# Linear attention and two feed-forward layers: q and k turned by VectorE's block transposes, projected as 32-row tiles in four single PSUM banks

## The chip, the cores and the metric

The kernel runs on one core of a Trainium2 chip. A core has a matrix engine (TensorE, PE in the profile, with PEld for its weight loads), a vector engine (VectorE, DVE), an activation engine (ScalarE, ACT), a general engine (GpSimd, POOL) and a queue engine that here only starts transfers (SyncE, SP). Each runs its own list of instructions in order and waits for the others at semaphores. Matmul results land in PSUM, which has eight banks of 128 x 512 fp32. The metric is the device time of one launch in microseconds (us).

## The reference

```
phi(x):  proj = x @ w_phi                       # 64 -> 128 features
         proj = proj - max|proj|  (per token)
         [exp(proj), exp(-proj)]
kv  = phi(k)^T v ;  z = sum phi(k)              # per batch (4) and head (8)
att = phi(q) kv / (phi(q) z + 1e-6)             # 576 tokens, head width 64
x   = att as (4*576) x 512
x   = (sigmoid(x w_gate) * (x w_val)) w_out     # 512 -> 1536 -> 512
out = max(0.01 h, h) w_out2,  h = x w_in2       # 512 -> 2048 -> 512
```

q, k, v and w_phi are fp32. The feed-forward weights come as 64-bit floats and are decoded on the chip into a high and a low part, and each product of these layers is three matmuls (`mm3`: high by high, high by low, low by high).

## The kernel before

**Stages.** The attention stage handles 16 pairs (a batch and two heads). Of a pair's 576 tokens, 512 are the main part, four tokens (J = 4) to a partition, and 64 are a remainder that two pairs share. After it comes the feed-forward stage; its first matmuls write `ps_u`. So that TensorE has more to do, the attention stage also takes in the first part of the gated layer for batches 0 to 2 (`gated_unit`, its chunk 0, 72 units M of three matmuls, written to `ps_g` and `ps_d`), and ten weight blocks are decoded in it (L104 to L111, five VectorE instructions each, tiles `e`, `m`, `raw`).

**A pair, step by step.** `load_kq`, `load_rem` and `load_v` fetch k, q, the remainder and v. TensorE transposes k and q, four 128 x 128 blocks each, into a PSUM pair of banks (`turn`, L408, `ps_t`); ScalarE or VectorE copies them to SBUF as x (L425, L428, and `evict` at L377 and L379, shared out by the string `XC`). `proj` (L396) multiplies x by w_phi: a head's 64 rows are one row tile, two heads stand in the array, and a matmul writes 128 columns of `ps_p`; `wbd` holds w_phi once for each head. VectorE takes the largest absolute value of each token (`absmax`, L383, 128 x 1024 for k and again for q) and subtracts it (`centre`, L388, tiles `t` and `tq`). ScalarE takes the two exponentials of k (`ka`, L455). TensorE transposes q's values (L500, L502, `ps_q`, `ps_r`) and ScalarE takes their exponentials (`qf`). `kv` (L526, L528) sums over the tokens, `kc` copies the sum to SBUF, and `om` (L545, L548, `ps_n`) multiplies it by q's features. `rc` and `nm` (L553 to L560) divide, `ot` (L573, L574, `ps_o`) transposes back, `xs` copies to `rb` (string `UC`), and `xh`, `xl` split it into high and low parts.

**Order.** The string `ORDER` lists the pieces, and under `manual_schedule` each engine gets its instructions in that order:

```
for piece in ORDER.split():
    nm = piece.rstrip("0123456789")
    if nm == "d": ...            # one step of a weight decode
    elif nm == "f": ...          # fetch the next raw weights
    elif nm in gated: gated[nm].popleft()()     # M t s h l c
    else: fns[nm](pair[int(piece[len(nm):])])
```

The eight warm-up matmuls on the identity (`ps_w`, L305 to L307) stand ahead of it.

**Banks.** Three pools of a pair of banks (`ps_p`, given out by the string `picks`) and two single banks (`ps_a`) serve the attention stage; the feed-forward stage opens pools of its own (L655 to L657).

## Time and profile before

| | us |
|---|---|
| median of 3 runs | 982.39 (981.71 to 983.8) |
| the profiled run's own time | 982.46 |
| its span in the trace | 980.7 |
| TensorE busy | 963.9 (98%) |
| VectorE busy | 732.1 (75%) |
| ScalarE busy | 470.6 (48%) |
| GpSimd busy | 166.6 (17%) |

The span is what the trace covers; 1.8 us of the profiled run lie around it. Busy times are sums over instructions. Matmuls overlap in the array, so what a run of matmuls takes is read from the start of one group to the start of the next, not from the duration of a record. An fp32 matmul leaves two records, so 16 matmuls read as x32.

### The profile page before, as it was taken

To read this page: it belongs to the slowest core of one execution; us is meant where nothing else is said; L and a number is where in the kernel's file an instruction comes from. 1 tells how busy PE (TensorE), PEld (TensorE's weight loads), DVE (VectorE), ACT (ScalarE), POOL (GpSimd) and SP (SyncE) were. 2 spreads that over 40 slices of the span, in tenths; PEclk is the share of its full clock that TensorE was granted. 3 is DMA by queue.
4 is the path that set the end of the run, shared out by engine and by line. 5 is a ranking of instruction groups with operands and counts; after the bars stand their busy time and mean duration, and the time that the engine had idled before them with its cause. 6 is when DMAs were issued, how large, how long until landed. Compare 5 with 4: busy or idle time off the path is not lost.

```text
span 980.7 us, 17543 instructions
## 1 busy us (share of the span) xinstructions
PE 963.9 (98%) x7040; PEld 820.7 (84%) x7040; DVE 732.1 (75%) x1226; ACT 470.6 (48%) x828; POOL 166.6 (17%) x228
## 2 busy tenths in 40 slices
PE   8999999999999999999999999999999999999998
PEld 7888889888888888888888887888888888888886
DVE  5898768625983838839839899987979797978545
...
GB/s 172 170 160 142 91 138 97 25 66 259 295 334 111 152 250 50 260 200 77 282 145 150 193 214 189 135 225 76 213 45 236 25 252 40 222 80 114 88 138 139
DMA packets 110177, 153.25 MB, mean 156 GB/s; under 512 B 62480, under 2 KB 65168, under 8 KB 110096
## 3 DMA queue, kind: packets, MB, share of 16 engines
...
## 4 chain that ended last, share of the span: by engine, by line
PE 76%; DVE 2%; issue 1%; POOL 0%; ACT 0%; DVEq 0%
PE ps_u L52 14%; PE ps_u L53 14%; PE ps_u L54 14%; PE ps_p L53 11%; PE ps_p L52 11%; PE ps_p L54 11%; DVE acc L738 1%; PE ps_n L545 0%; PE ps_d L52 0%; PE ps_g L52 0%; PE ps_g L54 0%; PE ps_g L53 0%; DVE w L807 0%; PE ps_d L53 0%; PE ps_d L54 0%
## 5 line engine op out<-in xcount | busy, mean ns | idle before, releaser
L908 DVE TENSOR_TENSOR q<-ps_u,q 128x512 f32<-128x512 f32 x160 | 109.6, 686 | 60.6 <-PE ps_u L54 54.1
L53 PE MATMUL ps_u<-xl,w 128*128 128x512 f32 (+1 forms) x432 | 151.4, 350 | 0.3 <-DVE xl L743 0.3
L52 PE MATMUL ps_u<-xh,w 128*128 128x512 f32 (+1 forms) x432 | 151.2, 350 | 0.0
L54 PE MATMUL ps_u<-xh,w 128*128 128x512 f32 (+1 forms) x432 | 151.1, 350 | 0.0
L978 DVE TENSOR_TENSOR acc<-acc,ps_p 128x512 f32<-128x512 f32 x126 | 86.1, 683 | 39.3 <-PE ps_p L54 38.7
L52 PE MATMUL ps_p<-w,gh 128*128 128x512 f32 x288 | 112.2, 390 | 0.0
L53 PE MATMUL ps_p<-w,gh 128*128 128x512 f32 x288 | 112.1, 390 | 0.0
L54 PE MATMUL ps_p<-w,gl 128*128 128x512 f32 x288 | 111.8, 389 | 0.0
L868 POOL DMA_DIRECT2D w<-td x88 | 48.5, 557 | 356.5 <-PE ps_u L54 344.7
L52 PE MATMUL ps_u<-w 128*128 128x512 f32 x256 | 100.2, 391 | 1.6 <-DVE q L908 1.6
L53 PE MATMUL ps_u<-w 128*128 128x512 f32 x256 | 99.9, 390 | 0.0
L54 PE MATMUL ps_u<-w 128*128 128x512 f32 x256 | 99.7, 389 | 0.0
L735 POOL DMA_DIRECT2D accd<-w x72 | 63.6, 894 | 189.5 <-ACT w L734 144.5
L53 PEld LDWEIGHTS ps_u<-xl,w 128*128 128x128 f32 x432 | 81.7, 189 | 11.7 <-DVE xl L743 0.5
L52 PEld LDWEIGHTS ps_u<-xh,w 128*128 128x128 f32 x432 | 81.7, 189 | 11.4
L54 PEld LDWEIGHTS ps_u<-xh,w 128*128 128x128 f32 x432 | 81.7, 189 | 10.9
L774 ACT ACTIVATE q<-q 128x512 f32<-128x512 f32 x48 | 30.2, 632 | 112.2 <-DVE q L908 112.1
L52 PE MATMUL ps_p<-gh,w 128*128 128x512 f32 (+1 forms) x216 | 78.3, 366 | 1.5 <-DVE acc L738 1.5
L53 PE MATMUL ps_p<-gl,w 128*128 128x512 f32 (+1 forms) x216 | 79.0, 366 | 0.0
L54 PE MATMUL ps_p<-gh,w 128*128 128x512 f32 (+1 forms) x216 | 78.9, 366 | 0.0
L49 DVE TENSOR_TENSOR gl<-q,gh 128x512 fp32r<-128x512 f32 (+1 forms) x102 | 61.9, 616 | 20.1 <-ACT gh L48 19.8
L48 ACT CAST gh<-q 128x512 fp32r<-128x512 f32 (+1 forms) x102 | 56.3, 561 | 17.3 <-DVE q L763 15.5
(131 smaller groups left out, 1921.1 us busy)
## 6 DMA issues: line engine op xcount, KB each, us to landing
...
```

What stands on the lines that cost most here:

```text
L48: nc.scalar.copy(hi, src)
L49: nc.vector.tensor_tensor(out=lo, in0=src, in1=hi.bitcast(F32), op=ALU.subtract)
L52: nc.tensor.matmul(ps, lh, rh, start=first, stop=False, **kw)
L53: nc.tensor.matmul(ps, lh, rl, start=False, stop=False, **kw)
L54: nc.tensor.matmul(ps, ll, rh, start=False, stop=last, **kw)
L735: nc.gpsimd.dma_start(out=accd[b][:, e], in_=st, accum_op=ALU.add)
L738: nc.vector.tensor_tensor(out=a, in0=a, in1=po, op=ALU.add)
L774: nc.scalar.activation(out=th, in_=t, func=ACTF.Lrelu)
L868: nc.gpsimd.dma_start(out=ts[n][k][0].bitcast(F32), in_=td[l, pair, n][:, k])
L908: nc.vector.tensor_tensor(out=o, in0=x, in1=y, op=ALU.add)
L978: nc.vector.tensor_tensor(out=a, in0=a, in1=po, op=ALU.add)
```

## The change

- k and q come into one tile `p.nat`. VectorE's 32 x 32 block transposes turn them (`xk` and `xq` for pair 0, `xx`, L422, for the others): 128 x 1024 elements in one instruction, from SBUF to SBUF, an element written every 16 bytes. TensorE's transposes of k and q and the copies of x are gone.
- After a block transpose the 32 rows of a tile hold half of a head's width for a quarter of the tokens. `proj` therefore makes 32 matmuls of 32 rows per pair, in four row tiles, each writing a bank of its own (`psa[g]`); two of them add up to one product. `wq` holds w_phi, and a copy with its halves swapped.
- The largest values and the subtractions go bank by bank (`rmax`, L380, and `less`, L449): eight instructions of 128 x 512 per pair instead of four of 128 x 1024.
- PSUM is eight single banks, named by `picks` and kept for the feed-forward stage too. What used a pair of banks (`ps_q`, `ps_n`, `ps_o`, `ps_g`, `ps_d`) now uses single ones, so `qa` and `nm` come in halves, `rc` has one add more, and `xs` two copies.
- v is loaded by two DMAs per head instead of one for both heads and one per head for the remainder. Pair 0's v and remainder go by ACT's queue. Output rows are written without a stride.
- `ORDER` is new, with the same number of decode steps, fetches and M's.

```diff
@@ gated_unit
             if i == kk == 0:
-                state["ps", f] = pair_bank("ps_g")
+                state["ps", f] = [None, None]
+            if kk == 0:
+                state["ps", f][i] = one_bank(512, "ps_g")
...
@@ pools
-    ps_p = [att.enter_context(tc.tile_pool(name=f"ps_p{i}", bufs=1, space=PS)) for i in range(3)]
-    ps_a = att.enter_context(tc.tile_pool(name="ps_a", bufs=2, space=PS))
-    picks = iter('0210210210210210120012012012021021021202020020201212112212020201021010210120120102121221212121201201210202101')
+    ps_a = ctx.enter_context(tc.tile_pool(name="ps_a", bufs=1, space=PS))
...
-    def pair_bank(name):
-        return ps_p[int(next(picks))].tile([128, 2, 512], F32, tag="pp", name=name)
+    nc.gpsimd.memset(wbd, 0.0)
+    wq = wk.tile([128, 2, NF], F32, name="wq")
 
     def one_bank(w, name):
-        return ps_a.tile([128, 512], F32, tag="at", name=name, bufs=2)[:, :w]
+        return ps_a.tile([128, 512], F32, tag="b" + next(picks), name=name)[:, :w]
...
@@ loads
+        p.nat = ld.tile([128, 2, J, 2, D], F32, tag="kq", name="kq")
+        for i, src in enumerate((k, q)):
+            t = p.nat[:, i]
...
+                if i == 0:
+                    eng.dma_start(out=wq[64 * h:64 * h + 64, 0], in_=w_phi)
...
-        nc.sync.dma_start(
-            out=vf[:, 0:J].rearrange("p j (h w) -> p j h w", h=2)[:, :, :, 0:64],
-            in_=v[b, 2 * c:2 * c + 2, 0:MAIN, :].rearrange("h (p j) d -> p j h d", j=J),
-        )
         for h in range(2):
-            nc.sync.dma_start(out=vf[64 * h:64 * h + 64, J, 66 * h:66 * h + 64], in_=v[b, 2 * c + h, MAIN:S])
+            eng.dma_start(out=vf[:, 0:J, 65 * h:65 * h + 64], in_=v[b, 2 * c + h, 0:MAIN, :].rearrange("(j p) d -> p j d", j=J))
+            eng.dma_start(out=vf[64 * h:64 * h + 64, J, 66 * h:66 * h + 64], in_=v[b, 2 * c + h, MAIN:S])
...
@@ projection and turn
-    def proj(x):
-        ps = pair_bank("ps_p")
-        for j in range(J):
-            for h in range(2):
-                rows = slice(64 * h, 64 * h + 64)
-                nc.tensor.matmul(ps[:, h, 128 * j:128 * j + 128], x[rows, 128 * j:128 * j + 128], wbd[rows, h * NF:(h + 1) * NF], start=True, stop=True)
-        return ps.rearrange("p h (j f) -> p (h j) f", j=J)
+    def proj(p, i):
+        if p.psa is None:
+            p.psa = [one_bank(512, "ps_a") for _ in range(4)]
+        for h in range(2):
+            for a in range(2):
+                for g in range(4):
+                    rows = slice(32 * g, 32 * g + 32)
+                    c0 = 256 * i + 128 * h
+                    nc.tensor.matmul(
+                        p.psa[g][:, c0:c0 + 128], p.x[rows, i, 2 * h + a],
+                        wq[rows, (a + g) % 2], start=a == 0, stop=a == 1, tile_position=(32 * g, 0),
+                    )
...
-    def turn(p, i, ps=None):
-        ps = p.ps if ps is None else ps
-        src = nat.pop(("kq"[i], p.i))
-        for j in range(J):
-            nc.tensor.transpose(ps[:, i, 128 * j:128 * j + 128], src[:, j].rearrange("p h d -> p (h d)"), ident)
...
-    def xc(p):
-        p.x = xt.tile([128, 2, MAIN], F32, tag="x", name="x", bufs=1)
-        evict(XC[p.i], p.x, p.ps)
+    def xk(p):
+        p.x = xt.tile([128, 2, 4, 32 * J], F32, tag="x", name="x", bufs=1)
+        nc.vector.transpose(out=p.x[:, 0].rearrange("p c (r j) -> p j c r", j=J), in_=p.nat[:, 0].rearrange("p j h (a d) -> p j (h a) d", a=2))
+        for g in range(4):
+            o = 32 * (g ^ 1)
+            (nc.gpsimd if g % 2 else nc.vector).tensor_copy(wq[32 * g:32 * g + 32, 1], wq[o:o + 32, 0])
+        for h in range(2):
+            rows = slice(64 * h, 64 * h + 64)
+            nc.gpsimd.tensor_copy(wbd[rows, h * NF:(h + 1) * NF], wq[rows, 0])
+        nc.scalar.activation(out=warm, in_=ebias, func=ACTF.Exp)
+
+    def xq(p):
+        nc.vector.transpose(out=p.x[:, 1].rearrange("p c (r j) -> p j c r", j=J), in_=p.nat[:, 1].rearrange("p j h (a d) -> p j (h a) d", a=2))
+
+    def xx(p):
+        p.x = xt.tile([128, 2, 4, 32 * J], F32, tag="x", name="x", bufs=1)
+        nc.vector.transpose(out=p.x.rearrange("p i c (r j) -> p i j c r", j=J), in_=p.nat.rearrange("p i j h (a d) -> p i j (h a) d", a=2))
...
+    def pp(p):
+        proj(p, 0)
+        proj(p, 1)
+
+    def rmax(p, g):
+        p.m[g] = absmax(p.psa[g].rearrange("p (c f) -> p c f", f=NF), f"{g}")
+
+    def less(p, g):
+        if p.t is None:
+            p.t = wk.tile([128, J, 2, 2, NF], F32, tag="t", name="t")
+        nc.vector.tensor_tensor(
+            out=p.t[:, g].rearrange("p i h f -> p (i h) f"), in0=p.psa[g].rearrange("p (c f) -> p c f", f=NF),
+            in1=p.m[g].unsqueeze(2).to_broadcast([128, 4, NF]), op=ALU.subtract,
+        )
...
@@ features, outputs
-        nc.scalar.activation(out=q_feat(p)[s][:, :, 0:MAIN], in_=p.ps, func=ACTF.Exp, scale=scales[s])
+        for h in range(2):
+            nc.scalar.activation(out=q_feat(p)[s][:, h, 0:MAIN], in_=p.ps[h], func=ACTF.Exp, scale=scales[s])
...
+        for n in range(2):
+            units = p.psn[n].rearrange("p (u w) -> p u w", u=2)
+            nc.vector.tensor_scalar_add(p.r[:, 4 * n:4 * n + 4].rearrange("p (j h) -> p j h", h=2), units[:, :, 64:66], 1e-6)
+        nc.vector.tensor_scalar_add(p.r[:, 8:10], p.psn[0][:, 130:195:64], 1e-6)
         nc.vector.reciprocal(p.r, p.r)
...
+                out=p.tn[:, 2 * n:2 * n + 2], in0=units[:, :, 0:132].rearrange("p j (h w) -> p j h w", h=2)[:, :, :, 0:64],
+                in1=p.r[:, 4 * n:4 * n + 4].rearrange("p (j h) -> p j h", h=2).unsqueeze(3).to_broadcast([128, 2, 2, D]), op=ALU.mult,
...
-        evict(UC[p.i], p.rb, p.ps.rearrange("p b t -> p (b t)")[:, 0:S])
+        evict(UC[p.i], p.rb[:, 0:MAIN], p.ps)
+        evict(UC[p.i], p.rb[:, MAIN:S], p.psr)
...
-    XC = "DAAADAAADDADDDAA"
-    UC = "DADADDDADADDAAAA"
+    UC = "DAADAAAADDDAAAAA"
     ORDER = """
-        lk0 lr0 lv0 ta0 xa0 tb0 lk1 pk0 xb0 lv1 pq0 rk0 tr0 sk0 lk2 xr0 pkr0 rq0 pqr0 lr2 ea0 eb0 sq0 rv0 tt1 f ru0 sv0 f su0
...
+        lk0 lk1 lr0 lv1 lv0 xk0 f pk0 xq0 f pq0 lk2 f rh0 tr0 sh0 xr0 lr2 rg0 pkr0 rb0 pqr0 sb0 rv0 sv0 sg0 ra0 sa0 ru0 ea0 su0
...
@@ banks of the stage after
-    ps_b = [ctx.enter_context(tc.tile_pool(name=f"ps_b{i}", bufs=1, space=PS)) for i in range(4)]
-    bank_order = [(ps_b[i // 2], f"b{i % 2}") for i in (4, 5, 6, 7, 0, 1, 2, 3)]
-    banks = {"u": bank_order[:5], "p": bank_order[5:]}
+    banks = {"u": [(ps_a, f"b{i}") for i in (6, 2, 1, 4, 0)], "p": [(ps_a, f"b{i}") for i in (7, 5, 3)]}
```

How the order changes is shown at three places. First TensorE's start. `ps_w` are the warm-up matmuls, `ps_tr` and `ps_pr` belong to the remainder. Before:

```order
L307 MATMUL ps_w<-ident 128x128 x8
L408 MATMUL ps_t<-ident,k 128x128 x4
L408 MATMUL ps_t<-ident,q 128x128 x4
L396 MATMUL ps_p<-wbd,x 128x128 x16
L437 MATMUL ps_tr<-ident,kr 128x128
L437 MATMUL ps_tr<-ident,qr 128x128
```

After:

```order
L396 MATMUL ps_a<-wq,x 128x128
L305 MATMUL ps_w<-ident 128x128 x8
L396 MATMUL ps_a<-wq,x 128x128 x31
L427 MATMUL ps_tr<-ident,kr 128x128
L427 MATMUL ps_tr<-ident,qr 128x128
L403 MATMUL ps_pr<-wbd,xr 128x256 x2
```

The transposes of k and q are gone, and one projection matmul now stands ahead of the warm-ups, 31 behind them.

Second, VectorE between the outputs of two pairs, early in the stage (`raw`, `m`, `e` are of the weight decode). Before, around pair 3's projection:

```order
L383 TENSOR_REDUCE m<-ps_p 128x8
L388 TENSOR_TENSOR t<-ps_p,m 128x1024
L107 SCALAR_TENSOR_TENSOR m<-raw,m 128x512
L108 SCALAR_TENSOR_TENSOR e<-raw,e 128x512
L109 SCALAR_TENSOR_TENSOR m<-m,e 128x512
L383 TENSOR_REDUCE m<-ps_p 128x8
L388 TENSOR_TENSOR tq<-ps_p,m 128x1024
L553 TENSOR_SCALAR r<-ps_n 128x8
L554 TENSOR_SCALAR r<-ps_n 128x2
L555 RECIPROCAL r<-r 128x10
L560 TENSOR_TENSOR tn<-ps_n,r 128x512
L104 TENSOR_SCALAR e<-raw 128x512
```

After, from pair 4's subtractions to the turn of pair 5:

```order
L107 SCALAR_TENSOR_TENSOR m<-raw,m 128x512
L449 TENSOR_TENSOR t<-ps_a,m 128x512 x4
L108 SCALAR_TENSOR_TENSOR e<-raw,e 128x512
L109 SCALAR_TENSOR_TENSOR m<-m,e 128x512
L380 TENSOR_REDUCE m<-ps_a 128x4 x4
L548 TENSOR_SCALAR r<-ps_n 128x4 x2
L549 TENSOR_SCALAR r<-ps_n 128x2
L550 RECIPROCAL r<-r 128x10
L556 TENSOR_TENSOR tn<-ps_n,r 128x256 x2
L422 STREAM_TRANSPOSE x<-kq 128x2x4x128
```

The reductions and subtractions of 1024 columns have become four and four of 512, and the turn stands behind the pair's outputs, in VectorE's own list.

Third, TensorE around the projection of pair 4 in the kernel before, with the two transposes of k and q that it needs:

```order
L574 MATMUL ps_o<-ident_131,tr_134 128x64
L401 MATMUL ps_pr<-wbd,xr 128x256
L408 MATMUL ps_t<-ident,k 128x128 x4
L408 MATMUL ps_t<-ident,q 128x128 x4
L500 MATMUL ps_q<-ident,tq 128x128 x8
L502 MATMUL ps_r<-ident,tqr 128x128
L401 MATMUL ps_pr<-wbd,xr 128x256
L396 MATMUL ps_p<-wbd,x 128x128 x16
L545 MATMUL ps_n<-kvz,qf 64x65 x32
L548 MATMUL ps_n<-kvz,qf 64x65 x4
L408 MATMUL ps_t<-ident,k 128x128 x4
L408 MATMUL ps_t<-ident,q 128x128 x4
```

After, from the last kv ahead of pair 5's projection to the output product behind it:

```order
L520 MATMUL kv<-vf_135,ka 64x65 x16
L522 MATMUL kv<-vf_135,kar 64x130 x2
L569 MATMUL ps_o<-ident,tn 128x128 x4
L571 MATMUL ps_or<-ident_123,tr_126 128x64
L493 MATMUL ps_q<-ident,t 128x128 x8
L495 MATMUL ps_r<-ident,tqr 128x128
L403 MATMUL ps_pr<-wbd,xr 128x256
L427 MATMUL ps_tr<-ident,kr 128x128
L427 MATMUL ps_tr<-ident,qr 128x128
L396 MATMUL ps_a<-wq,x 128x128 x32
L539 MATMUL ps_n<-kvz,qf 64x65 x32
```

Nothing stands in place of the transposes; the projection is 32 matmuls, in one piece for k and q.

## Rows read from the trace of the kernel before

**Rows 1.** Busy time by stretch; stretch, its length, each engine's busy us (instructions), granted clock, DMA.
```profile
core 0: us, PE busy (x) PEld busy (x) DVE busy (x) ACT busy (x) POOL busy (x), PEclk, DMA share, GB/s
30.00:60.00 30.00, 28.34 (x571) 25.59 (x572) 28.12 (x45) 22.61 (x42) 6.14 (x6) 1.00 0.62 153
60.00:227.00 167.00, 162.89 (x2511) 143.04 (x2510) 110.27 (x169) 102.05 (x194) 30.46 (x32) 1.00 0.38 100
227.00:981.00 754.00, 746.23 (x3576) 628.50 (x3574) 575.89 (x986) 328.72 (x565) 124.89 (x170) 1.00 0.57 168
```

**Rows 2.** VectorE's waits, 0 to 227 us; what waited for what: total us, times, longest.
```profile
DVE m L383 <- PE ps_p L396: 20.5, 11, 6.4
```

**Rows 3.** TensorE in order of time, the start; start us, us, engine, line, tiles.
```profile
1.48 3.59 PE L307 MATMUL ps_w<-ident 128*128 128x128 f32 x16 [1.48 <-POOL ident masks.py:199]
4.90 0.60 PE L408 MATMUL ps_t<-ident,k 128*128 128x128 f32 x4
...
6.39 2.05 PE L396 MATMUL ps_p<-wbd,x 64*128 64x128 f32 x32
```

**Rows 4.** VectorE in order of time, 0 to 28 us.
```profile
7.60 1.22 DVE L383 TENSOR_REDUCE m<-ps_p 128x8 f32<-128x1024 f32 x1 [6.42 <-PE ps_p L396]
...
10.00 1.21 DVE L383 TENSOR_REDUCE m<-ps_p 128x8 f32<-128x1024 f32 x1
...
12.39 0.74 DVE L383 TENSOR_REDUCE m<-ps_pr 128x2 f32<-128x256 f32 x2
...
21.48 0.42 DVE L104 TENSOR_SCALAR e<-raw 128x512 int32<-128x512 int32 x1
...
22.27 0.69 DVE L107 SCALAR_TENSOR_TENSOR m<-raw,m 128x512 f32<-128x512 uint32 x1
23.47 0.17 DVE L553 TENSOR_SCALAR r<-ps_n 128x8 f32<-128x8 f32 x1 [0.50 <-PE ps_n L548]
...
23.98 0.69 DVE L560 TENSOR_TENSOR tn<-ps_n,r 128x512 f32<-128x512 f32 x1
24.59 0.68 DVE L108 SCALAR_TENSOR_TENSOR e<-raw,e 128x512 int32<-128x512 int32 x1
25.31 0.69 DVE L109 SCALAR_TENSOR_TENSOR m<-m,e 128x512 f32<-128x512 f32 x1
```

**Rows 5.** Instructions by line and form, 0 to 225 us; busy us, mean ns, idle before.
```profile
L379 DVE COPY x<-ps_t 128x1024 f32<-128x1024 f32 x6 | 7.3, 1220 | 4.3 <-PE ps_t L408 4.1
```

**Rows 6.** TensorE in order of time, one pair's pieces.
```profile
21.10 2.09 PE L545 MATMUL ps_n<-kvz,qf 128*64 128x65 f32 x64
...
23.25 1.10 PE L526 MATMUL kv<-vf,ka 128*64 128x65 f32 x32
...
25.66 0.66 PE L573 MATMUL ps_o<-ident,tn 128*128 128x128 f32 x4
...
26.32 1.04 PE L500 MATMUL ps_q<-ident,tq 128*128 128x128 f32 x8
...
27.31 0.60 PE L401 MATMUL ps_pr<-wbd,xr 128*128 128x256 f32 x2
27.84 2.06 PE L396 MATMUL ps_p<-wbd,x 64*128 64x128 f32 x32
29.83 0.70 PE L401 MATMUL ps_pr<-wbd,xr 128*128 128x256 f32 x2
30.36 0.60 PE L408 MATMUL ps_t<-ident,k 128*128 128x128 f32 x4
30.80 0.60 PE L408 MATMUL ps_t<-ident,q 128*128 128x128 f32 x4
```

**Rows 7.** TensorE in order of time, a unit M and the stage's end.
```profile
200.27 0.39 PE L52 MATMUL ps_d<-gh,w 128*128 128x512 f32 x1
...
200.96 0.39 PE L52 MATMUL ps_d<-gh,w 128*128 128x512 f32 x1
...
226.62 0.40 PE L52 MATMUL ps_u<-xh,w 128*128 128x512 f32 x1
```

More of the change, by code (lines that the diff above doesn't have):

```diff
@@ L338, in load_kq @@
                 eng.dma_start(out=t[:, :, h], in_=src[b, h, 0:MAIN, :].rearrange("(p j) d -> p j d", j=J))
-                if nm == "k":
-                    eng.dma_start(out=wbd[64 * h:64 * h + 64, h * NF:(h + 1) * NF], in_=w_phi)
-        if p.i == 0:
-            nc.scalar.activation(out=warm, in_=ebias, func=ACTF.Exp)
+                if i == 0:
+                    eng.dma_start(out=wq[64 * h:64 * h + 64, 0], in_=w_phi)
     def load_rem(p):
         b, c = p.b, p.c
+        eng = nc.sync if p.i else nc.scalar
         for nm, src in (("k", k), ("q", q)):
@@ L496, in qf @@
     def qf(p):
-        p.ps = pair_bank("ps_q")
+        p.ps = [one_bank(512, "ps_q") for _ in range(2)]
         for h in range(2):
             for j in range(J):
-                nc.tensor.transpose(p.ps[:, h, 128 * j:128 * j + 128], p.tq[:, J * h + j], ident)
+                nc.tensor.transpose(p.ps[h][:, 128 * j:128 * j + 128], p.t[:, j, 1, h], ident)
         p.psr = one_bank(128, "ps_r")
@@ L525, in kv @@
                 for cs in COLS:
-                    nc.tensor.matmul(ps[cs, s, h], p.kf[:, s, J * h + j, cs], p.vf[:, j, 64 * h:64 * h + 65], start=(s, h, j) == (0, 0, 0), stop=False, skip_group_check=True)
+                    nc.tensor.matmul(ps[cs, s, h], p.kf[:, s, j, h, cs], p.vf[:, j, 64 * h:64 * h + 65], start=(s, h, j) == (0, 0, 0), stop=False, skip_group_check=True)
         for cs in COLS:
@@ L537, in om @@
     def om(p):
-        p.psn = pair_bank("ps_n")
-        units = p.psn.rearrange("p b (u w) -> p (b u) w", u=2)
+        p.psn = [one_bank(512, "ps_n") for _ in range(2)]
         for j in range(J):
@@ L558, in nm @@
         p.tn = wk.tile([128, J, 2, D], F32, tag="tn", name="tn")
-        units = p.psn.rearrange("p b (u w) -> p (b u) w", u=2)
-        nc.vector.tensor_tensor(
-            out=p.tn, in0=units[:, :, 0:132].rearrange("p j (h w) -> p j h w", h=2)[:, :, :, 0:64],
-            in1=p.r[:, 0:8].rearrange("p (j h) -> p j h", h=2).unsqueeze(3).to_broadcast([128, J, 2, D]), op=ALU.mult,
-        )
+        for n in range(2):
+            units = p.psn[n].rearrange("p (u w) -> p u w", u=2)
+            nc.vector.tensor_tensor(
+                out=p.tn[:, 2 * n:2 * n + 2], in0=units[:, :, 0:132].rearrange("p j (h w) -> p j h w", h=2)[:, :, :, 0:64],
+                in1=p.r[:, 4 * n:4 * n + 4].rearrange("p (j h) -> p j h", h=2).unsqueeze(3).to_broadcast([128, 2, 2, D]), op=ALU.mult,
+            )
     def nr(p):
         p.tr = trs[p.i % 2]
-        nc.scalar.activation(out=p.tr[COLS[0], 0:64], in_=p.psn[COLS[0], 0, 130:194], func=ACTF.Copy, scale=p.r[COLS[0], 9:10])
-        nc.scalar.activation(out=p.tr[COLS[1], 64:128], in_=p.psn[COLS[1], 0, 131:195], func=ACTF.Copy, scale=p.r[COLS[1], 8:9])
+        nc.scalar.activation(out=p.tr[COLS[0], 0:64], in_=p.psn[0][COLS[0], 130:194], func=ACTF.Copy, scale=p.r[COLS[0], 9:10])
+        nc.scalar.activation(out=p.tr[COLS[1], 64:128], in_=p.psn[0][COLS[1], 131:195], func=ACTF.Copy, scale=p.r[COLS[1], 8:9])
     def ot(p):
-        p.ps = pair_bank("ps_o")
+        p.ps = one_bank(512, "ps_o")
         for j in range(J):
-            nc.tensor.transpose(p.ps[:, 0, 128 * j:128 * j + 128], p.tn[:, j].rearrange("p h d -> p (h d)"), ident)
-        nc.tensor.matmul(p.ps[:, 1, 0:REM], p.tr, ident2, start=True, stop=True)
+            nc.tensor.transpose(p.ps[:, 128 * j:128 * j + 128], p.tn[:, j].rearrange("p h d -> p (h d)"), ident)
+        p.psr = one_bank(REM, "ps_or")
+        nc.tensor.matmul(p.psr, p.tr, ident2, start=True, stop=True)
     def xs_(p):
         p.rb = wk.tile([128, S], F32, tag="rb", name="rb", bufs=2)
-        evict(UC[p.i], p.rb, p.ps.rearrange("p b t -> p (b t)")[:, 0:S])
+        evict(UC[p.i], p.rb[:, 0:MAIN], p.ps)
+        evict(UC[p.i], p.rb[:, MAIN:S], p.psr)
     def x_parts(p):
@@ new lines, in linear_attention_moe @@
+        qb14 kv14 xs13 M xh13 pp15 qr14 xl13 eb14 d1 kw14 ra15 rh15 sh15 M kc14 sa15 om14 rg15 sg15 rb15 sb15 M rc14 ea15 nm14
+        qf15 eb15 s M d4 nr14 M qa15 d5 ot14 qb15 M M xs14 M xh14 M qr15 xl14 h kv15 d6 l t d7 kw15 M kc15 om15 s h l M rc15
+        nm15 M M nr15 c ot15 M xs15 M xh15 M c xl15 M c M c
+    """
+    fns = dict(lk=load_kq, lr=load_rem, lv=load_v, xk=xk, xq=xq, xx=xx, tr=tr, xr=xr, pk=pk, pq=pq, pp=pp, **{n + z: (lambda p, f=f, g=g: f(p, g)) for n, f in (("r", rmax), ("s", less)) for g, z in enumerate("abgh")}, ea=ea, eb=eb,
+               pkr=pkr, ru=rkr, su=skr, er=er, es=es, pqr=pqr, rv=rqr, sv=sqr, qf=qf, qr=qr, qa=qa, qb=qb, kv=kv, kw=kw, kc=kc,
```

110 lines of the change are left out of this document (40 added, 70 removed).

## The prediction, made before the changed kernel ran

> **What bounds the kernel now.** I read three views in this order: the busy time by stretch, the waits, and the engines' order of work in time. The stretches say which engine to count [rows 1]. From 227 us to the end, in the feed-forward stage, TensorE (PE in the rows) is busy 746.23 of 754 us. The change alters no instruction there except which bank it uses, so I cost that stage at nothing, and everything below is about the attention stage, which ends when the first `ps_u` matmul starts, at 226.62 us [rows 7]. Inside that stage there are two regimes. From 30 to 60 us VectorE (DVE) is busy 28.12 of 30 us and TensorE 28.34, so the two run neck and neck; from 60 to 227 us TensorE is busy 162.89 of 167 and VectorE only 110.27 [rows 1]. VectorE's largest wait in the stage, 20.5 us in 11 times, is for TensorE's projections, one of 6.4 us being the start [rows 2]. The reader should see from this that work taken off TensorE pays late in the stage, and work put onto VectorE costs early in it.
>
> **TensorE's work, before.** One pair's pieces stand one behind another between 21.10 and 30.80 us [rows 6]. From start to start: the output product (`ps_n`) 2.15 us, the two halves of kv 2.41, the output's transposes (`ps_o`) 0.66, the feature transposes (`ps_q`, `ps_r`) 0.99, one remainder projection (`ps_pr`) 0.53, the projection (`ps_p`) 1.99, and four transposes of k 0.44, so eight of k and q 0.88. Some 0.15 us per pair go to the remainder's transposes. That is 9.76 us per pair and 156.2 us for 16. A unit M of the gated layer (three matmuls) takes 200.96 − 200.27 = 0.69 us [rows 7], and 72 of them 49.7 us. Together 205.9 us of work lie in 226.6 us; the other 20.7 us are the start, waits and change-overs. From 60 us on TensorE's idle time is only 167 − 162.89 = 4.1 us [rows 1], so the larger part of the 20.7 lies early.
>
> **Part 1, the transposes go from TensorE.** 16 × 0.88 = 14.1 us of its work are removed, and nothing on TensorE replaces them.
>
> **Part 2, 32-row tiles.** A pair now needs 32 projection matmuls instead of 16, each fp32 matmul being two records, so 64 instead of 32. Now two 64-row tiles run beside each other, and a record costs 1.99/32 = 62 ns [rows 6], while a record of a full-height transpose costs 0.44/4 = 110 ns. Two tiles side by side therefore already come within an eighth of halving the time. If four tiles share the array as well as two do, a record costs 31 ns and the pair 1.99 us as before; if no more than two overlap, it costs 62 ns and the pair 3.97 us. I take 32 ns, close to the lower end because the rows show the overlap working nearly in full for two: 2.05 us a pair, +0.06, or +1.0 us over 16.
>
> On this the Trainium skill ("TensorE: Matmul & The Clock Gate", section "Packing small matmuls — row/col tiling") is less generous: it states a measured speed-up of 3.07 for four row tiles of K=32. By that factor on the 110 ns a record would be an estimated 36 ns and the pair 2.3 us, some 2.5 us more over the ten pairs behind pair 5; no run here shows it yet.
>
> So TensorE's work after is 205.9 − 14.1 + 1.0 = 192.8 us.
>
> **Part 3, VectorE takes the turns.** Prices from start to start [rows 4]: a 1024-wide reduce or subtract (12.39 − 10.00)/2 = 1.20 us; a 512-wide two-operand instruction (25.31 − 23.98)/2 = 0.67; a 256-wide reduce 0.74/2 = 0.37; the three small ones ahead of `tn` 0.51, so 0.17 each. A turn moves 128x1024 elements. No row shows a block transpose. The nearest is the copy of the same x from PSUM, 1.22 us busy [rows 5], and I take its price from start to start, 1.20. The lower end is an integer operation out of SBUF: two 512-wide ones in 22.27 − 21.48 = 0.79 us [rows 4], so 0.79 for 1024. The upper end is twice the copy, 2.4 us, since the turn writes single elements 16 bytes apart, and no row has such a write.
>
> The Trainium skill ("SBUF — State Buffer", section "Specifications (TRN2)") speaks against exactly this step: SBUF has lines of 16 bytes, wants two hits in a line for full bandwidth, and each crossing to a new line pays. By it every element the turn writes pays, which is the rival "dear turn" below; nothing in before's trace tests it.
>
> Over the stage VectorE gets 16 × 1.20 of turns and loses the 6 copies of x (7.2): +12.0. Splitting 32 reduces and 32 subtracts into halves costs 2 × 0.67 − 1.20 = 0.13 each, 64 times: +8.4. The halves of `tn` cost 2 × 0.37 − 0.61 = 0.13, 16 times +2.1, one more small add per pair 16 × 0.17 = +2.7, and three fewer copies of the output about −2. Together +23 us, on an engine that had 57 us free from 60 us on but nothing before. ScalarE loses nine copies of x and gets split exponentials; it was busy 102.05 of 167 us, and that hides it.
>
> **Part 4, the start.** Now the eight warm-up matmuls run from 1.48 us, while the loads are in flight, in 3.59 us for 16 records; the first transposes start at 4.90, the first projection at 6.39 and VectorE's first reduce at 7.60 [rows 3, 4]. In the new order one projection matmul stands ahead of the warm-ups, and it waits for the turn of k. The turn of k cannot start before k has landed, so it ends about where the transposes started, near 4.9. Then come the warm-ups, 3.6 us, and the other projections, 2.0: pair 0's banks are full at 10.4, and the first reduce starts near 10.5, 2.9 us later than now. Uncovered, because VectorE has nothing else to do there.
>
> **The sum.** I follow VectorE to the turn of pair 5 (L422, the fifth of them), because up to there it is the longer chain. Ahead of it and including it stand 20 reduces and 16 subtracts of 512 (36 × 0.67 = 24.1), five turns (6.0) and two half turns (1.3), ten remainder instructions (3.7), three weight decodes at 0.79 + 0.69 + 0.72 + 0.69 = 2.9 [rows 4] (8.7), three times the small ones (3 × 0.68 = 2.0), six halves of `tn` (2.2), an output copy (0.9) and two w copies (0.4): 49.3 us. Of them 1.7 (half turns, w copies) are done before 10.5. With 1.5 us allowed for its waits, pair 5's turn ends at 10.5 + 47.6 + 1.5 = 59.6, its projection at 61.6. TensorE has by then done six projections (12.3), four feature transposes (4.0), four kv (9.6), three outputs with transposes (8.4), six remainder projections (3.2) and 0.6 of remainder transposes: 38.1 us, no M yet. It stands 23.5 us behind its own work. What is left is 192.8 − 38.1 = 154.7 us, with the M's to fill it. I add 6 us for waits and change-overs, from the 4.1 idle now: 61.6 + 154.7 + 6 = 222.3, against 226.6. That is 4.3 us earlier: 982.46 − 4.3 ≈ 978 us. The profiled run (982.46) lies at the median of the runs (982.39), so no correction is needed.
>
> Other edits cost nothing. The gated unit's single banks leave its matmuls as they are. A pair's v comes in four DMAs instead of three, on SP, which only issues loads and is well ahead. Rows of the output are written contiguously in the stage that TensorE bounds.
>
> **Rivals.** *Fuller gain.* The turn costs 0.79, or VectorE catches up early because TensorE has less to give it. Were TensorE bound as now throughout, with the later start: 226.6 − 14.1 + 1.0 + 2 = 215.5, so 971 us. For it: from 60 us on TensorE alone is full. Against it: 30 to 60 us, where VectorE is full already and gets more.
>
> *Neck and neck to pair 9.* Per pair VectorE needs 8 × 0.67 + 1.20 + 0.74 + 0.68 + 0.74 = 8.7 and, while decodes last, 2.9 more: 11.6. TensorE needs 8.9 and some three M's, 11.0. Where neither has slack, every wait of one is lost for both: about 1 us in each of the pairs 5 to 9, so 983, no change. For it: the balance just worked out. Against it: M's are there to shift.
>
> *Overlap only in twos* (the slower side). Every projection then takes 3.97 us. Ahead of pair 5 TensorE has slack, from pair 6 on it has none: 10 pairs × 1.92 = 19 us, giving 978 + 19 = 997. It decides as soon as a record costs over some 39 ns (4.3 us over ten pairs). For it: no row shows more than two tiles; against it: two overlap nearly fully.
>
> *Dear turn.* At 2.4 us, six turns' worth ahead of pair 5's projection add 7.2 us, a little more behind: about 986, slower as well.
>
> **Chances.** Forecast (975 to 980.4) 0.43; fuller gain (967 to 975) 0.14; neck and neck (980.4 to 984.4) 0.20; twos 0.08; dear turn 0.15. About 2 us (0.2%) is what a measurement of this kernel can tell from no change. Faster 0.57, same 0.20, slower 0.23. The range 968 to 992 takes in the dear turn and the start of the twos; the likeliest case alone is 975 to 980.4.
>
> **What would show it.** In the new trace: the turn L422 at 1.2 us; a burst of 64 projection records in about 2.05 us; the first reduce near 10.5 us; pair 5's projection near 60; the first `ps_u` near 222. A first `ps_u` after 226 with TensorE waiting for VectorE behind pair 5 means neck and neck; bursts of 4 us mean twos; turns of 2 us or more mean the dear turn.

## The result, and the profile after

The changed kernel takes 996.9 us (median of 4 runs, 995.9 to 997.5), against 982.2 in the same session: a ratio of 1.0146, 95% interval 1.0129 to 1.0164. It is slower by 14.7 us. The forecast was 978, its range 968 to 992; the miss is 18.9 us. The spans of the two traces are 995.7 and 980.7 us.

The busy time by stretch of the changed kernel, columns as in [rows 1]; the last two stretches are split where its attention stage ends:

```profile
core 0: us, PE busy (x) PEld busy (x) DVE busy (x) ACT busy (x) POOL busy (x), PEclk, DMA share, GB/s
12.00:30.00 18.00, 12.92 (x223) 11.46 (x223) 15.09 (x25) 7.01 (x15) 0.00 (x0) 0.72 0.60 157
30.00:60.00 30.00, 22.66 (x437) 20.47 (x436) 28.39 (x51) 16.93 (x37) 7.00 (x6) 0.89 0.56 139
60.00:237.00 177.00, 171.80 (x3118) 149.01 (x3115) 137.36 (x271) 110.82 (x247) 33.54 (x36) 0.99 0.38 100
237.00:995.00 758.00, 749.27 (x3579) 630.11 (x3577) 576.31 (x986) 328.02 (x564) 124.72 (x168) 1.00 0.57 167
```

TensorE (PE) had 28.34 busy us between 30 and 60 us before [rows 1]; it now has 22.66, and 12.92 of 18 ahead of that, much of it at the lower of the two clock levels (1.2 instead of 2.4 GHz: a granted clock of 0.72 is a mixture of 1.00 and 0.5). Pair 3's projection, for one, comes behind 3.86 us of idle time and runs at a granted clock of 0.54. VectorE (DVE) is the full engine there, 28.39 of 30. The first `ps_u` of the feed-forward stage, at 226.62 us before [rows 7], stands here:

```profile
237.40 0.39 PE L52 MATMUL ps_u<-xh,w 128*128 128x512 f32 x1
```

So the attention stage grew by 10.8 us, and the rest of the span (995.7 − 237.4 = 758.3, before 980.7 − 226.62 = 754.1) by 4.2.

The changed lines, grouped by line over the attention stage (busy us, mean ns of one, idle before and its releasers):

```profile
L396 PE MATMUL ps_a<-wq,x 32*128 32x128 f32 x1024 | 42.8, 305 | 15.1 <-DVE x L422 5.4 <-DVE x L408 5.3 <-DVE t L449 2.1
L449 DVE TENSOR_TENSOR t<-ps_a,m 128x512 f32<-128x512 f32 x64 | 42.3, 683 | 1.6
...
L422 DVE STREAM_TRANSPOSE x<-kq 128x1024 f32<-128x1024 f32 x15 | 31.2, 2078 | 0.0
```

A turn of 1024 elements to a partition takes 2078 ns. The copy of x that it was priced by took 1220 [rows 5]. The start, TensorE in order of time, and VectorE's first reduction:

```profile
5.26 0.79 PE L396 MATMUL ps_a<-wq,x 32*128 32x128 f32 x2 [5.26 <-DVE x L408]
5.98 3.35 PE L305 MATMUL ps_w<-ident 128*128 128x128 f32 x16
9.26 2.06 PE L396 MATMUL ps_a<-wq,x 32*128 32x128 f32 x62
```

```profile
11.38 0.69 DVE L380 TENSOR_REDUCE m<-ps_a 128x4 f32<-128x512 f32 x1 [4.15 <-PE ps_a L396]
```

As forecast, one projection matmul waits for the turn of k, then come the warm-ups, then the other projections, and the first reduction starts at 11.38 us instead of 7.60 [rows 4] (forecast 10.5).

From there VectorE works to the turn of pair 5 with four waits, 5.81 us in all, three for projections and one for the output product:

```profile
24.04 1.29 DVE L380 TENSOR_REDUCE m<-ps_a 128x4 f32<-128x512 f32 x2 [2.56 <-PE ps_a L396]
...
49.56 2.48 DVE L380 TENSOR_REDUCE m<-ps_a 128x4 f32<-128x512 f32 x4 [1.20 <-PE ps_a L396]
...
61.00 2.48 DVE L380 TENSOR_REDUCE m<-ps_a 128x4 f32<-128x512 f32 x4 [0.94 <-PE ps_a L396]
64.60 0.23 DVE L548 TENSOR_SCALAR r<-ps_n 128x4 f32<-128x4 f32 x2 [1.11 <-PE ps_n L542]
```

The projection of pair 5 was forecast to start at 59.6 us. First VectorE from the turn on, then TensorE's projections of pair 4 (without its first matmul) and pair 5:

```profile
65.85 2.09 DVE L422 STREAM_TRANSPOSE x<-kq 128x1024 f32<-128x1024 f32 x1
67.79 0.41 DVE L104 TENSOR_SCALAR e<-raw 128x512 int32<-128x512 int32 x1
68.13 0.39 DVE L106 TENSOR_SCALAR m<-raw 128x512 int32<-128x512 int32 x1
68.55 0.69 DVE L107 SCALAR_TENSOR_TENSOR m<-raw,m 128x512 f32<-128x512 uint32 x1
69.16 0.68 DVE L449 TENSOR_TENSOR t<-ps_a,m 128x512 f32<-128x512 f32 x1
69.76 0.41 DVE L380 TENSOR_REDUCE m<-ps_pr 128x2 f32<-128x256 f32 x1
70.09 0.68 DVE L449 TENSOR_TENSOR t<-ps_a,m 128x512 f32<-128x512 f32 x1
```

```profile
57.00 4.38 PE L396 MATMUL ps_a<-wq,x 32*128 32x128 f32 x62 [0.95 <-DVE t L449]
...
70.83 2.98 PE L396 MATMUL ps_a<-wq,x 32*128 32x128 f32 x64 [0.49 <-DVE t L449]
```

The turn ends at 67.9, yet the projection starts at 70.83. What it waits for last is named at its end: pair 4's subtractions (L449), which must empty the banks. On VectorE they stand behind the turn, and a weight decode's three steps (L104, L106, L107) stand between. But TensorE stands still for only 1.0 us of these 2.9 (0.53 ahead of the remainder's transposes and the 0.49 above, both for L449); until 69.4 us it still works off what stands ahead of the projection in its own list. The lower clock had made that list late: the projection of pair 4, above, took 4.38 us at a granted clock of 0.50, where at the full clock 64 records take 2.07.

At the start of the feed-forward stage, first ScalarE's first tanh, in the kernel before and here, then TensorE:

```profile
232.00 0.60 ACT L761 ACTIVATE q<-ps_u 128x512 f32<-128x512 f32 x1 [3.85 <-DMA accd<-st]
```

```profile
245.33 0.60 ACT L757 ACTIVATE q<-ps_u 128x512 f32<-128x512 f32 x1 [6.39 <-DMA accd<-st]
```

```profile
253.66 0.50 PE L52 MATMUL ps_p<-gh,w 128*128 128x512 f32 x1 [1.61 <-ACT gh L48]
254.56 0.80 PE L53 MATMUL ps_p<-gl,w 128*128 128x512 f32 x1 [0.39 <-DVE gl L49]
255.15 0.63 PE L54 MATMUL ps_p<-gh,w 128*128 128x512 f32 x1
```

The tanh waited 6.39 us for the last store of the gated unit's sums (`accd<-st`), since its buffer takes over that memory. Before, it waited 3.85 us for the same store and TensorE did not wait at all; now the tanh comes 7.9 us behind the first `ps_u`, instead of 5.4. The hidden tiles come late, TensorE waits 1.6 and 0.4 us and comes back at the lower clock (0.59 us from the second of these rows to the third; the granted clock is 0.72 from 254 to 260 us).

### The profile page after: what moved, and what is told of

Same layout as the page of the kernel before. It is cut to its first block, busy times and chain, and to the rows that moved or that the text cites. A ratio compares the mean times of both kernels' runs of the same rounds, so it can differ in the third digit from the quotient of the medians.

```text
span 995.7 us, 18470 instructions
## 1 busy us (share of the span) xinstructions
PE 963.1 (97%) x7424; PEld 816.8 (82%) x7424; DVE 760.5 (76%) x1336; ACT 464.5 (47%) x863; POOL 168.8 (17%) x233
## 4 chain that ended last, share of the span: by engine, by line
PE 85%; DVE 10%; DMA 2%; ACT 1%; issue 1%; POOL 0%; SPq 0%; DVEq 0%; ACTq 0%
PE ps_u L52 13%; PE ps_u L53 13%; PE ps_u L54 13%; PE ps_p L53 11%; PE ps_p L54 11%; PE ps_p L52 11%; PE ps_a L396 3%; PE ps_n L539 2%; PE kv L520 2%; DVE m L380 2%; DVE t L449 2%; DVE x L422 1%; PE ps_g L52 1%; DMA accd<-st 1%; PE ps_q L493 1%
```

## The experiments

Two ideas run through the experiments: that VectorE's early chain with a dear turn sets the pace (A), or that the new order and the single banks do (C). All edits are to the changed kernel, but for e10. e1 leaves out what would put the tokens back in their order, and with it e5, e6, e9, e11 and e12; e9 leaves out twelve reductions besides. The amount of the other work stays. The table gives each kernel's time (median, ratio to the kernel before with its interval), the start of pair 5's projection, the first `ps_u`, and the span behind it, the last three from its trace. A trace is of one run: that of e7 and of e9 is some 2 us below the kernel's median, that of e2 and e6 some 2 us above.

| kernel | us | ratio | pair 5 | `ps_u` | behind |
|---|---|---|---|---|---|
| changed | 996.9 | 1.0146 (1.0129–1.0164) | 70.83 | 237.40 | 758.3 |
| e1 turn in runs of 32 | 988.1 | 1.0051 (1.0032–1.0069) | 65.77 | 230.28 | 756.2 |
| e2 turn on TensorE, ScalarE | 1009.5 | 1.0273 (1.0253–1.0292) | | 251.01 | 758.6 |
| e3 warm-ups first | 993.6 | 1.0109 (1.0094–1.0124) | 67.50 | 235.56 | 756.6 |
| e4 sums early at the end | 996.2 | 1.0136 (1.0121–1.0151) | 71.85 | 239.89 | 754.6 |
| e5 = e1 + e3 + e4 | 985.6 | 1.0035 (1.0024–1.0046) | 63.98 | 228.45 | 755.1 |
| e6 = e5 + filling | 989.7 | 1.0071 (1.0058–1.0084) | 63.80 | 228.98 | 760.4 |
| e7 as e2, better start | 1003.1 | 1.0212 (1.0199–1.0225) | 66.79 | 243.41 | 755.7 |
| e8 as e5, tokens put right | 1002.0 | 1.0203 (1.0189–1.0216) | 70.38 | 245.27 | 755.9 |
| e9 = e5, 12 reductions fewer | 982.3 | 1.0005 (0.9996–1.0014) | 58.95 | 223.41 | 755.0 |
| e10 before, turn in pairs 7–15 | 991.3 | 1.0096 (1.0082–1.0110) | | 236.49 | 754.3 |
| e11 = e1 + e3 | 987.2 | 1.0041 (1.0028–1.0054) | 66.22 | 230.73 | 755.6 |
| e12 = e1 + e4 | 987.3 | 1.0054 (1.0042–1.0066) | 66.08 | 230.56 | 754.9 |

**e1, the turn's output step.**

```diff
-        p.x = xt.tile([128, 2, 4, 32 * J], F32, tag="x", name="x", bufs=1)
-        nc.vector.transpose(out=p.x.rearrange("p i c (r j) -> p i j c r", j=J), in_=...)
+        p.x = xt.tile([128, 2, 4, J, 32], F32, tag="x", name="x", bufs=1)
+        nc.vector.transpose(out=p.x.rearrange("p i c j r -> p i j c r"), in_=...)
```

> Only the turn's output step is changed: blocks are written as 32 consecutive elements instead of one element every 16 bytes (tokens then stand in another order inside a 128-token group, and k's features meet v's rows in that other order: part of the result differs, the amount of work does not). Theory A (VectorE's chain bounds the stage up to about pair 8, and the turn costs 2.08 us because of its 16-byte steps): the turn falls to about 1.2 us, pair 5's projection comes 5 to 6 us earlier, first ps_u near 230, about 989 us. Theory B (a block transpose of 1024 elements costs 2 us however it is written): turn stays at 2.0 to 2.1, time 996 to 998. Theory C (the new order and the single banks cost the time, not the turn): the turn falls, but the time stays above 994.

The turns in e1, by line:

```profile
L422 DVE STREAM_TRANSPOSE x<-kq 128x1024 f32<-128x1024 f32 x15 | 18.5, 1231 | 0.0
...
L408 DVE STREAM_TRANSPOSE x<-kq 128x512 f32<-128x512 f32 x1 | 0.7, 712 | 3.4 <-DMA kq<-in_k_dram 3.4
```

Theory A was right nearly to the number: 1231 ns instead of 2078, the time 988.1. Pair 5's projection moves from 70.83 to 65.77, 5.1 us. The five turns give 4.2 of them. VectorE's waits shrink by 1.9 (5.81 to 3.94), but the first reduction comes 0.55 later, at 11.93, so the two half turns' saving does not show. So up to there the turns' saving arrives in full. From pair 5 to the first `ps_u` another 2.1 us go, and 2.1 behind it. B, as the expectation has it, falls.

What e1 leaves is 10 us over the forecast. VectorE's rows show where the early part lies: the first reduction, two waits for projections, the fifth turn, and pair 4's first subtraction behind it:

```profile
11.93 0.69 DVE L380 TENSOR_REDUCE m<-ps_a 128x4 f32<-128x512 f32 x1 [5.31 <-PE ps_a L396]
...
24.01 1.29 DVE L380 TENSOR_REDUCE m<-ps_a 128x4 f32<-128x512 f32 x2 [2.73 <-PE ps_a L396]
...
48.07 2.48 DVE L380 TENSOR_REDUCE m<-ps_a 128x4 f32<-128x512 f32 x4 [1.21 <-PE ps_a L396]
...
61.56 1.23 DVE L422 STREAM_TRANSPOSE x<-kq 128x1024 f32<-128x1024 f32 x1
...
64.08 0.68 DVE L449 TENSOR_TENSOR t<-ps_a,m 128x512 f32<-128x512 f32 x1
```

From the first reduction (11.93) to the end of the fifth turn (62.79) pass 50.9 us, of which 2.73 and 1.21 are waits; 46.9 us are work, against 47.6 in the forecast. The sum of VectorE's work was right once the turn is cheap. Late are the start (1.4 us), the waits (3.9 instead of 1.5), and again the step from the turn's end to the projection, 3.0 us. Here too TensorE stands still for only 0.7 of them, and works off its own list in the rest:

```profile
65.77 2.98 PE L396 MATMUL ps_a<-wq,x 32*128 32x128 f32 x64 [0.51 <-DVE t L449]
```

**e2 and e7, the turn given back to TensorE.**

```diff
-        nc.vector.transpose(out=p.x..., in_=p.nat...)
+        for j in range(J):
+            nc.tensor.transpose(ps[:, 128 * j:128 * j + 128], p.nat[:, i, j].rearrange("p h d -> p (h d)"), ident)
+        nc.scalar.copy(p.x[:, i], ps)          # e7: on VectorE for pair 0
```

> The turn is given back to TensorE (8 transposes per pair into two single banks) and to ScalarE (two copies of 512 per pair), and the projection uses two 64-row tiles as before; the eight single banks, the splits into 512 and the order are kept as changed (some turns stand a few pieces later, where two banks are free). Theory A: VectorE loses 33 us of turns, the early starvation goes away, TensorE's stage is 14 us longer in work than planned: first ps_u near 228 to 231, 987 to 991 us. Theory C (order, splits and single banks): 995 or more, as TensorE only got more work.

The fence shows the core of the edit; the 64-row projection and the order of v's and the output's rows go back to the kernel before with it. Theory A missed by 20 us, and the number is C's. Part was the experiment's own: pair 0's copy of x stood on ScalarE behind the loads of its queue and the table load,

```profile
9.73 1.28 ACT L408 ACT_TABLE_LOAD   x1 [9.73 <-DMA vf<-in_v_dram]
11.02 0.59 ACT L408 COPY x<-ps_t 128x512 f32<-128x512 f32 x1
```

so e7 mended the start.

> As e2_pe_turn, but pair 0's two copies of x on VectorE, which is idle then, because in e2 they stood on ScalarE behind its load issues until 9.7 us, and warm-ups first. Theory A2 (turns on TensorE cost their 0.88 us per pair in full, since from 30 us on TensorE is the longer chain as soon as VectorE has no turns): e2 less its late start of about 6 us, so 1002 to 1004, still slower than the changed kernel's 996.9. Rival (e2 was slow for its start alone, with the half clock that came of it): 995 or less.

It is within its expectation: 1003.1. Even dear, the turn on VectorE is better than TensorE's transposes in this order, by 6 us, and by 9.5 against e3 below, which has the same warm-ups. Up to pair 5 the two are nearly level (66.79 against 67.50 in e3), although e7 has taken all turns off VectorE, which is busy only 23.66 of the 30 us from 30 to 60 us in it. So the early part does not hang on the sum of VectorE's work alone. With the transposes on TensorE, as in the kernel before, the new order, the splits and the single banks end the stage at 243.4 instead of 226.6. That leaves room for C, but it is no price of the order and the banks: e7 gives ScalarE all copies of x but pair 0's, and TensorE's largest wait in it, 5.1 us in 4 times, is for ScalarE's exponentials of k; its transposes take two more banks per pair in an order that was not laid out for them.

**e3, the start.** The warm-ups are moved into the ordered part, ahead of the first piece.

> The eight warm-up matmuls stand ahead of every projection matmul again; nothing else. Theory A (VectorE's chain from its first reduce to pair 8 is what counts): the first reduce comes at about 8.2 instead of 11.4 us and the whole stage moves up by about 2.5 to 3.2 us: 994. Rival (the start is made up for by later slack): first reduce earlier, the time the same within 1 us.

993.6, 3.3 us less; VectorE's first reduction comes at 8.61 instead of 11.38, pair 5 3.3 us earlier. Up to there the late start is paid in full. Of that, 1.8 us are left at the first `ps_u`; the stage behind it is 1.7 shorter as well, which the expectation did not have.

**e4, the end of the order.**

```diff
-        nm15 M M nr15 c ot15 M xs15 M xh15 M c xl15 M c M c
+        nm15 M M nr15 c ot15 M M c M xs15 c M xh15 M c xl15
```

> Only the end of the order is changed: the four output sums of the gated unit (pieces c) each stand right behind the matmuls they need, ahead of the last pair's xs, xh, xl, so the last store of the sums is issued ahead of the load of acc. Theory: the feed-forward stage's 4.2 us come from ScalarE's first tanh waiting 6.4 us for that store, TensorE then waiting 2.0 us for its hidden tiles and running 9 matmuls at half clock: all of it goes, about 993 us (996.9 - 4). Rival (the feed-forward stage is longer because of its new banks): first tanh earlier, the time the same.

The trace is the theory's, the time the rival's. The tanh waits 3.85 us, as in the kernel before, TensorE's waits at the start of the feed-forward stage are gone, and that stage is 3.7 us shorter (754.6). But the time fell by 0.7, within the intervals. In its profile the attention stage is 2.5 us longer, from the very start, which the edit does not touch: the warm-ups and pair 0's projection ran longer (in the changed kernel the projection starts at 9.26 and takes 2.06). The granted clock reads 1.00 there in both traces, so what lengthened them is open:

```profile
9.76 3.17 PE L396 MATMUL ps_a<-wq,x 32*128 32x128 f32 x62
```

e11 and e12 ask again with the cheap turn.

> e5_contig_warm_tail without its edit of the end: turn in runs of 32 (part of the result differs), warm-ups first, the changed kernel's own end of the order. Theory (the stall at the start of the feed-forward stage, 3 to 4 us in the traces of the changed kernel, is paid in every run): 2 to 4 us slower than e5's 985.6, so 988 to 989. Rival (the stall is worth little in the time, as e4's 0.7 us says): 985 to 986.

> e1_contig with the edit of the end, warm-ups where the change has them. Theory (stall paid in full): 988.1 - 3.7 = 984.5. Rival (worth little): 987 to 988. Beside e5 it also gives the price of the late warm-ups with the cheap turn: 2.5 to 3.3 us if the early chain carries it, as in e3.

By medians the end of the order is worth 1.6 us (e11 to e5) and 0.8 (e1 to e12); the late warm-ups, with the cheap turn, 0.9 to 1.8 (e1 to e11, e12 to e5). The intervals overlap in all four comparisons, so none of these prices is clear of noise; the stall that looks like 4.2 us in one trace is small in the time. e11's runs spread from 983.7 to 989.1; in its profile the projections of pairs 3 and 4 take 3.80 and 4.03 us where e5's take 2.07 and 3.20, although the two kernels differ only behind them. So the clock in the early pairs differs from run to run, and the time goes with it: e11's four runs at a mean granted clock of 0.995 took 983.7 to 984.7 us, its seven at 0.990 to 0.994 took 985.5 to 989.1.

**e5, the three together.**

> The three edits that each took time back, together: turn written in runs of 32 elements (part of the result differs, as in e1_contig), warm-up matmuls first, output sums early at the end. Theory A (the three are separate terms: 8.8 us for the turn's step, 3.3 for the start, and the 3.7 us of the feed-forward stage's stall that e4's trace shows gone): 988.1 - 3.3 - 3.7 = 981, the same as before. Rival (they overlap: what one frees, the clock or TensorE's other waits take): 985 or more, as e4 alone gave only 0.7 us.

985.6: the rival's number. Of the last two terms, 7.0 us together, 2.5 came. With all three the kernel is still 0.35% slower than before, and 7.6 us over the forecast.

**e6, filling TensorE's gaps.**

```diff
+            for _ in range({1: 4, 2: 8, 3: 16, 4: 10, 5: 8, 6: 8, 7: 6}.get(p.i, 0)):
+                nc.tensor.matmul(p.psa[0][:, 0:128], ident, ident, start=True, stop=True)
```

> As e5_contig_warm_tail, and 78 matmuls on the identity more, issued where TensorE waits for VectorE in pairs 0 to 7 (18 ahead of pair 0's feature transposes, 4 to 16 ahead of the projections of pairs 1 to 7), into banks that are overwritten. Theory (the half clock after each early starvation is a cost of its own): the granted clock stays at full from 12 to 60 us, projections there take 2.1 instead of 3.1 to 3.8 us, and the time falls by 2 to 4 us against e5. Rival (VectorE's chain bounds these pairs whatever TensorE's clock): within 1 us of e5, or slower by the 78 matmuls that delay it.

The stretches of e5, then of e6:

```profile
12.00:30.00 18.00, 13.73 (x298) 11.90 (x298) 14.88 (x29) 9.36 (x18) 0.70 (x1) 0.81 0.69 179
30.00:60.00 30.00, 23.87 (x516) 21.37 (x516) 27.98 (x53) 16.30 (x36) 7.13 (x7) 0.94 0.57 145
```

```profile
12.00:30.00 18.00, 16.73 (x345) 15.71 (x344) 16.72 (x32) 9.87 (x19) 1.27 (x1) 1.00 0.75 192
30.00:60.00 30.00, 29.61 (x595) 27.57 (x593) 28.85 (x56) 17.51 (x40) 6.54 (x6) 1.00 0.54 144
```

The clock did stay at full, and the time rose by 4 us. But in the trace the attention stage is level with e5's (228.98 against 228.45), and the loss lies behind it, 760.4 against 755.1. There the tanh waits no longer than in e5 (3.88 and 3.75 us), and VectorE's first decode step waits for a weight load that lands 3.6 us later; first e5, then e6:

```profile
234.36 0.43 DVE L104 TENSOR_SCALAR e<-raw 128x512 int32<-128x512 int32 x1 [10.81 <-DMA raw<-in_moe_w_out_dram]
```

```profile
237.97 0.43 DVE L104 TENSOR_SCALAR e<-raw 128x512 int32<-128x512 int32 x1 [13.89 <-DMA raw<-in_moe_w_out_dram]
```

TensorE then waits 2.2 and 0.5 us for hidden tiles. Why the load comes later is not shown. So the time does not settle the clock's price. Inside the attention stage the filling stood behind the wait for the banks and delayed what it should have helped. In TensorE's order in e6 the eight filling matmuls of pair 5 and then its projection are:

```profile
61.82 2.05 PE L390 MATMUL ps_a<-ident 128*128 128x128 f32 x16 [0.52 <-DVE t L449]
63.80 2.07 PE L396 MATMUL ps_a<-wq,x 32*128 32x128 f32 x64
```

The first bank was free at 61.82, some 2 us before e5's projection at 63.98, and the filling took those 2 us. By that estimate the lower clock costs about 2 us up to pair 5.

**e8, the tokens put right.** v in eight DMAs per pair, q's transposes by a permuted identity.

> As e5_contig_warm_tail with the full computation: v comes in the tokens' new order (eight DMAs of 32 partitions per pair instead of two), and q's feature transposes multiply by a permuted identity, which puts the tokens back. Theory: both are off the path (SP only issues loads; the matmul replaces the transpose one for one): within 1.5 us of e5. Rival: the eight DMA issues, some 0.5 us each, hold up SP's other loads early, and the stage waits for them: 2 us or more slower than e5.

The rival came true, but it is not the whole of the 16.4 us. SP's issues of v, and of `kr` for pairs 2 and 3 behind them (`kr` was issued at 15.10 in the changed kernel), then the TensorE wait that followed:

```profile
5.68 4.37 SPq L360 DMA_DIRECT2D vf<-in_v_dram  x8
...
11.37 3.90 SPq L360 DMA_DIRECT2D vf<-in_v_dram  x8
...
23.01 1.26 SPq L347 DMA_DIRECT2D kr<-in_k_dram  x2
```

```profile
28.84 0.44 PE L430 MATMUL ps_tr<-ident,kr 128*128 128x128 f32 x1 [5.70 <-DMA kr<-in_k_dram]
```

With this wait, pair 5's projection starts 6.4 us later than in e5 (70.38 against 63.98). The other 10.4 us come behind it: from there to the first `ps_u` e8 takes 174.9 us and e5 164.5, and DMAs hold up TensorE for only 1.0 us of that. What is dear there is the permuted identity, which the expectation took to replace the transpose one for one. One pair's q in e8, then in e5:

```profile
80.39 1.95 PE L496 MATMUL ps_q<-perm,t 128*128 128x128 f32 x16
```

```profile
73.99 1.04 PE L491 MATMUL ps_q<-ident,t 128*128 128x128 f32 x8
```

As ordinary matmuls the eight leave sixteen records instead of eight and take 0.9 us more; eleven of the sixteen pairs have them behind pair 5's projection, which makes 10 us.

So e1 and e5 are no kernels to use as they stand: putting their tokens right in this way costs more than the cheap turn gives.

**e9, less on VectorE.**

```diff
+        if p.i < 6 and len(p.m) % 2:
+            p.m[g] = list(p.m.values())[-1]
+            return
```

> As e5_contig_warm_tail, and in pairs 0 to 5 two of the four largest-value reductions (128x512) are left out, their banks taking the largest value of the bank before: 12 instructions, 8 us less on VectorE, all of them early (part of the result differs). Theory A (VectorE's chain sets the pace up to pair 5 one for one, TensorE's surplus is only used behind it): pair 5's projection starts 6 to 7 us earlier than in e5 (57 instead of 64 us), first ps_u about 222 to 224 instead of 228.5, and the time is about 979 to 981 (e5 985.6). Rival (what bounds the early pairs is the chain of waits through projection, largest value, exponential, kv and output, not the sum on VectorE): pair 5's projection moves by 3 us or less, 983 or more.

```profile
58.95 2.98 PE L394 MATMUL ps_a<-wq,x 32*128 32x128 f32 x64 [0.69 <-DVE t L450]
```

Pair 5 and the stage's end both move by 5.0 us (63.98 to 58.95, 228.45 to 223.41), the time, by medians, by 3.3. Between the two expectations, nearer to A: ten of the twelve reductions, 6.7 us, stand ahead of pair 5's projection, and three quarters of that arrive there. All that arrives there arrives at the stage's end: from pair 5's projection to the first `ps_u` e1, e5 and e9 each take 164.5 us, and TensorE is busy for 162.1 of them. A version without these 12 reductions is level with the kernel before.

**e10, the turn only late.** The kernel before, with cheap turns and 32-row tiles in pairs 7 to 15, pairs of banks and 1024-wide reductions kept.

> The kernel before, its order, pairs of banks and 1024-wide reductions kept, with the change's turn and 32-row projection in pairs 7 to 15 only, where VectorE has time: block transposes written in runs of 32, k loaded so that the tokens keep their places (eight DMAs per pair), k and q of a pair projected into two pairs of banks, the exponentials of k in two halves. The full computation. Theory A (TensorE's 0.88 us per pair are worth their full price where TensorE alone is the bound, and the change lost them by loading VectorE early): 9 x 0.88 = 7.9 us less, 974 to 977 us. Rival (VectorE's turn in front of each projection makes TensorE wait there too, since order and banks were laid out for transposes on TensorE): 980 to 985.

The rival, and worse than it said. TensorE's largest waits in e10, and its stretch from 60 us to the stage's end:

```profile
PE ps_q L547 <- DVE tq L402: 6.6, 6, 2.1
PE ps_n L594 <- DVE t L402: 3.2, 3, 2.7
```

```profile
60.00:236.00 176.00, 160.51 (x2718) 138.20 (x2719) 113.51 (x181) 99.27 (x206) 29.45 (x32) 0.98 0.35 93
```

TensorE is idle for 176 − 160.5 = 15.5 us where the kernel before idled 4.1 in 167 [rows 1]: k's projection had to move behind to q's place, and all that follows it came late. The 0.88 us per pair aren't had by putting the turn into an order made without it.

## Why the prediction was wrong

**TensorE's prices** were right at the full clock. The transposes are gone, and from pair 8 on, but for pair 9, 64 projection records take 2.07 us, 32 ns each, as taken; the rival "overlap only in twos" did not come, though its 997 us did, by luck. Its sign, bursts near 4 us, did stand in the trace: pairs 1, 3 and 4 took 3.6 to 4.4 us. There the granted clock was 0.50 to 0.54, so it was the clock and not the overlap. (The Trainium skill, "TensorE: Matmul & The Clock Gate", section "Packing small matmuls — row/col tiling", states a speed-up of 3.07 for four row tiles, at 512 columns; 110 ns for a full-height record against 32 is 3.4 here, at 128 columns, so the measurement decides.)

**Part 3, the turn's price, is the step that failed first.** I took 1.20 us, by the copy's row; it is 2.08, near the upper end of 2.4. The rival "dear turn" had named the mechanism, and e1 shows it: with only the output step changed the turn takes 1.23. By the medians of e1 and the changed kernel that is 8.8 us of the 18.9. (The Trainium skill's rule on 16-byte lines, "SBUF — State Buffer", section "Specifications (TRN2)", pointed the right way; the trace agrees, 2078 ns against 1231.) The rival priced it at 986, because it counted six turns ahead of pair 5 and only "a little more behind"; e1 gives back 4.2 us there.

**The sum to pair 5 left out what stands between the turn and the projection.** I let pair 5's projection start when its turn ends. It also needs banks, and these are freed by pair 4's subtractions, which the new order puts on VectorE behind the turn and a decode's steps. The order shown ahead of the prediction is headed "from pair 4's subtractions to the turn of pair 5", and that is a misreading: the four subtractions in it are pair 3's (at 56.27 us in the trace, ahead of pair 4's reductions at 61.00). And I took TensorE to have worked off by then all that stands ahead of the projection in its own list; it had not. From the turn's end to the projection pass 2.9 us, of which TensorE stands still for 1.0.

The 11.2 us by which pair 5 was late are the start (0.9 us later than said), VectorE's work (50.7 us instead of 47.6: the five turns 4.4 more, the rest 1.3 less), its waits (5.8 instead of the 1.5 allowed, partly because projections at the lower clock take up to 4.4 us), and these 2.9. The rival "neck and neck" had the mechanism of the waits, each engine in turn waiting for the other, but put it at pairs 5 to 9; in the trace it lies ahead of pair 5.

**Behind pair 5** the stage took 166.6 us instead of 162.7, in part the turn again (e1 takes 2.1 of the 3.9 away).

**"That stage costs nothing"** failed too: I looked for changed instructions in the feed-forward stage and not at what its first one waits for. The order's end stores the last sum after the load of acc, and that stage is 4.2 us longer in the profile; by the medians the edit gave back 0.7 to 1.6, which is not clear of the intervals.

**Still open:** with the cheap turn, the early start and the new end, e5 is still 3.5 us above the kernel before and 7.6 above the forecast, so no run shows the gain that was forecast. How this divides among the split reductions, the single banks and the order is open, as it is for e7's 17 us. e9 shows that less early work on VectorE helps, e7 that taking off all the turns, at the price of TensorE's transposes and ScalarE's copies, does not; no run undoes the splits alone. The price of the lower clock is an estimate.
